# A fused attention and SwiGLU kernel: k and q of the fourth unit load ahead of the first weight slice, and the second slice loads and converts over more units

## The chip, the cores and the metric

The kernel runs on one core of a Trainium2 chip. Its engines are TensorE (PE, with its weight loads PEld), VectorE (DVE), ScalarE (ACT), GpSimd (POOL) and SyncE (SP), which here does nothing but start transfers. The metric is the device time of one execution in microseconds (us); lower is better.

## What is computed

Attention with a sigmoid in place of the softmax, over 4 batches of 12 heads, 448 tokens, 64 numbers a head; its result, as 1792 tokens of 768 numbers, goes through a root-mean-square norm and a SwiGLU layer. q, k and v are 32-bit floats; the weights arrive as 64-bit floats.

```python
def _attn_ref(q, k, v):
    scale = 1.0 / np.sqrt(q.shape[-1])
    scores = scale * np.matmul(q, k.transpose(0, 1, 3, 2)) - np.log(q.shape[2])
    return np.matmul(1.0 / (1.0 + np.exp(-scores)), v)

def _moe_ref(x, w_gate, w_val, w_out, rms_g):      # x: 1792 x 768
    xn = x / np.sqrt(np.mean(x * x, -1, keepdims=True) + 1e-06) * rms_g
    g = xn @ w_gate                                # 768 x 1536
    return (g / (1.0 + np.exp(-g)) * (xn @ w_val)) @ w_out
```

## The kernel before

**Attention.** The work is cut into 12 units, each of four heads of one batch (three units a batch), and each unit into 7 chunks of keys. The main loop (L897 to L919) takes two chunks a step, n = 0, 2, 4 and so on up to 84: `scores` (L265: 12 matmuls and one sigmoid on ACT for each chunk), then `av` (L284: 4 matmuls, each of two passes) of the two chunks before them. So unit u begins at chunk 7u. Below, "scores 4.0" is the first chunk of unit 4, and units count from 0: the fourth unit is unit 3.

**What a unit needs.** q and k are loaded as floats (`load_qk`, L191: two transfers of 224 KB each for q and two for k), split on DVE into a high and a low half of 16 bits (`qk_hi` L221, `qk_lo` L225), and transposed into `t_b`. Units 0 and 1 are transposed on PE; so is q of unit 2 (`on_pe`: matmuls at L257 into a PSUM tile `tr`, copied out by ACT at L262 and DVE at L260). From unit 3 on, and for k of unit 2, a DMA transposes them (L228, L234). `FILL` (L849) says in which chunk each of these steps is issued: while unit u computes, unit u + 2 is split and transposed, v of unit u + 1 and k and q of unit u + 4 are loaded. A matmul tile for `tr`, for `av`, for the norm's sums and for the later products comes from the same ring of four PSUM banks (`ps_m`), so a `tr` matmul waits until the one four banks earlier has been copied out.

**Weights.** The gate and value matrices are cut into 6 slices of 256 columns, 768 KB for each matrix of a slice. `load_w` (L451) queues three transfers a matrix (one of 384 KB and two of 192 KB); `run_load` (L458) starts the next one of that queue. `split_w` (L462) converts a slice: for each matrix three DVE passes over 64-bit words (L436, L437, L438), then four differences (L488), the 16-bit high half on ACT (L491) and the low half on DVE (L494). Its first list (`first`) has for slices 0 and 1 the gate's four entries, then the value's four and the differences; the last pass of a matrix queues the loads of the next slice, since its room is then free. `wr` in the profile is the room of the weights, `xc` holds loads of q and k, `t_b` and later the normed tokens.

**What sets the order.** Three lists (`adds`, `norms`, `splits`) are worked off by `run_later` (L797) within a credit for DVE and ACT that grows with every chunk; a part of `splits` runs only when nothing of the first two stands ready. The sums of squares are added on DVE (L314) and summed on PE (`ssq`, L346); the norm of a batch is then a row of small DVE instructions (L351 to L371), two spreads (L374), a product on PE (`rinv`, L384) that ACT copies (L385), the scaling (L388), sums (L410) and splits of the scaled tokens (L392, L395, L399). What is left at the end of attention is issued in a fixed number of parts before and within the first products.

**Transfers.** All of them are started by SP, in the order of the program. Eight completion semaphores are used in turn, so a transfer is started only when the one eight places ahead of it has landed, and when the room that it writes is free.

**After attention** come 24 blocks of products with the weights (`quad`, L535, matmuls at L524, tiles cb, cd, ca) and the products with w_out (L727), in which PE goes from one matmul to the next.

Of the kernel before, what the change touches and what calls it, by code (L numbers as in the profile page):

```python
# [24 lines left out]
def attention_then_swiglu(  # L25
# [42 lines left out]
    ps_m = ctx.enter_context(tc.tile_pool(name="ps_m", bufs=4, space=bass.MemoryType.PSUM))  # L68

    WARM, BETWEEN = 6, 2  # L70
    SPLIT_AT, REST_AT = (8, 30), 12
    LOADS_FROM = 10
    PIECES = (0, 4), (4, 3)
    MID = 3
    SLOT = 0.8
# [109 lines left out]
    def load(src, dst, u):  # L185
        b, n = divmod(u, NPAIR // 2)
        for r in range(2):
            rows = src[b, 4 * n + 2 * r : 4 * n + 2 * r + 2].rearrange("h s d -> (h s) d")
            nc.sync.dma_start(dst[:, r], rows.rearrange("(p c) d -> p c d", p=P))  # L189

    def load_qk(u, t):  # L191
        load((q, k)[t], (raw_b if u < 2 else ld_b)[u % 2][:, t], u)
# [13 lines left out]
    def g_columns():  # L206
        ps = bank("g")
        nc.tensor.matmul(ps[:, :NCC], g_row, ident[:NCC, :NCC], start=True, stop=True)
        nc.vector.tensor_copy(g_sb.rearrange("p (c o) -> p o c", o=2), ps[:, :NCC].rearrange("p (o c) -> p o c", o=2))
# [55 lines left out]
    def scores(u, c):  # L265

        T = t_b[u % 3]
        ps = banks("sc")

        for n, (l, m) in enumerate(PARTS):  # L270
            for r in range(2):
                rows = slice(D * r, D * r + D)
                for j in range(2):
                    cols = slice(PB * j, PB * j + PB)
                    o = ps[cols, r, :S].rearrange("p (c x) -> p c x", c=NSLOT)
                    nc.tensor.matmul(  # L276
                        o, T[rows, 1, l, c, cols], T[rows, 0, m, :, cols], start=(n == 0), stop=(n == 2)
                    )
        a = at[u, c] = a_b[(u * NSLOT + c) % 4]
        nc.scalar.activation(  # L280
            a, ps[:, :, :S], AF.Sigmoid, bias=-math.log(S), scale=1.0 / (math.sqrt(D) * SQ * SQ)
        )
# [39 lines left out]
    def run_evictions(n):  # L322
        for part in evictions[:n]:
            part()
        del evictions[:n]
# [123 lines left out]
    loads = []  # L449

    def load_w(fc, kind):  # L451


        src = swapped((w_gate, w_val)[kind][:, 2 * fc * P : 2 * fc * P + 2 * P])
        dst = raw_w[kind].rearrange("p c f w -> p c (f w)")
        loads.extend((fc, lambda d=d, x=x: nc.sync.dma_start(d, x)) for d, x in zip(sides(dst), src))

    def run_load():  # L458
        if loads:
            loads.pop(0)[1]()  # L460
# [331 lines left out]
    adds, norms, splits = [], [], []  # L792
# [4 lines left out]
    def run_later():  # L797
        calls[0] += 1
        credit[0] = min(credit[0] + SLOT, 2.5)
        credit[1] = min(credit[1] + ACT_SLOT, 0.6)  # L800
        for queue in (adds, norms, splits):
            while queue:
                part, cost, *on_act = queue[0]
                if part is wait:
                    if cost <= calls[0]:
                        queue.pop(0)
                    break
                if credit[bool(on_act)] <= 0:
                    break
                queue.pop(0)  # L810
                part()
                credit[bool(on_act)] -= cost
# [12 lines left out]
    K, Q = 1, 0  # L825
# [40 lines left out]
    with tc.manual_schedule():  # L866
# [16 lines left out]
        load_v(1)  # L883
        load_w(0, 0)
        load_w(0, 1)
        for t in (K, Q):
            for _ in range(3):
                run_load()
            load_qk(3, t)

        transpose_here(0, Q)
        warm(BETWEEN)
# [3 lines left out]
        split = {}  # L896
        for n in range(0, len(todo) + 2, 2):  # L897
            for u, c in todo[n : n + 2]:
                scores(u, c)
                run_evictions(1)  # L900
                for part in FILL[c]:
                    part(u)
                if n == 6 and c == 6:
                    g_columns()
                run_later()
            for u, c in todo[max(n - 2, 0) : n]:
                av(u, c)
                run_evictions(1)
                run_later()
            for _ in range(n // LOADS_FROM):  # L910
                if loads and loads[0][0] < 2:
                    run_load()
            if n in SPLIT_AT:
                fc = SPLIT_AT.index(n)
                split[fc] = split_w(fc)
                first, second = split[fc]
                splits.extend(first[:4] if fc == 0 else first + second)
            if n == REST_AT:
                splits.extend(split[0][0][4:] + split[0][1])  # L919
        run_evictions(len(evictions))  # L920


# [46 lines left out]
        for fc, n in order:  # L969
# [5 lines left out]
            elif fc + 1 < NFC:  # L975
                first, second = split[fc + 1] = split_w(fc + 1) if n == 0 else split[fc + 1]
# [97 lines left out]
```

## Time and profile before

| | |
|---|---|
| median of 3 runs | 575.09 us (572.03 to 577.34) |
| the profiled execution | 576.98 us, of which the span of its instructions 575.2 us |
| PE busy | 563.9 us (98%), 4230 matmuls |
| DVE, ACT busy | 437.8 us (76%), 265.9 us (46%) |
| transfers | 87.25 MB, mean 152 GB/s |

The span is what lies between the first and the last instruction; about 1.8 us of the execution lie around it. All times below are counted from the start of the span. PE busy is the sum of its matmuls at whatever clock was granted. The page also gives the granted TensorE clock in 40 slices of the span; all but the third show 9 tenths of full speed (the third shows 8).

### The profile page before, as it was taken

The page shows a single profiled execution, that of the slowest core. Times are in us where ns is not written, and L with a number is a line of the kernel's source. Part 1 is how long each engine was busy: PE and PEld are TensorE (multiplying, and loading weights), DVE is VectorE, ACT ScalarE, POOL GpSimd, SP SyncE. Part 2 cuts the span into 40 slices and gives each one's busy share as a digit, 9 for nine tenths or more (in the row PEclk, how much of TensorE's full clock was granted, in tenths as well). Part 3 has the DMA queues.
Part 4 walks back from the last instruction along what each step waited for, and adds up shares of the span by engine and source line. Part 5 has one row for each costly group of instructions (what it writes and reads, how often), then busy time and mean ns, then how long its engine had stood idle before and what let it go on. Part 6 is the DMA issues. An engine that isn't in the chain of part 4 may idle for free.

```text
span 575.2 us, 10261 instructions
## 1 busy us (share of the span) xinstructions
PE 563.9 (98%) x4230; PEld 304.4 (53%) x4230; DVE 437.8 (76%) x576; ACT 265.9 (46%) x397; POOL 0.7 (0%) x6
## 2 busy tenths in 40 slices
PE   8979999999999999999999999999999999999997
PEld 6435454454555555555555555555556666666664
DVE  4597899998887777878778787787557987777751
ACT  5759698886454243342433424325438342222220
POOL 0000000000000000000000000000000000000000
PEclk9989999999999999999999999999999999999999
DMA  7999999881016357282573835632526566444211
GB/s 246 216 272 264 245 228 256 167 189 20 1 46 169 120 156 197 90 226 79 155 192 98 219 81 156 189 106 65 179 59 224 152 217 201 145 142 145 71 43 41
DMA packets 98417, 87.25 MB, mean 152 GB/s; under 512 B 38719, under 2 KB 91458, under 8 KB 98370
## 3 DMA queue, kind: packets, MB, share of 16 engines
q1 hardware_dynamic: 97810, 85.91, 57.0%
q8 instruction: 33, 0.54, 0.4%
q10 hardware_dynamic: 560, 0.69, 0.3%
q14 instruction: 14, 0.11, 0.1%
HBM read 61.34 MB, written 16.52 MB: 135 GB/s over the span
## 4 chain that ended last, share of the span: by engine, by line
PE 85%; DMA 6%; DVE 4%; ACT 2%; SPq 1%; issue 1%; DVEq 0%; ACTq 0%
PE cb L524 28%; PE cd L524 14%; PE oc L727 7%; PE o L727 7%; PE od L727 7%; PE ca L524 7%; PE av L291 6%; PE sc L276 4%; PE ob L727 4%; DMA xc<-room 2%; DMA xc<-in_q_dram 1%; DMA wr<-in_moe_w_gate_dram 1%; ACT room L280 1%; DMA room<-in_k_dram 1%; SPq L189 1%
## 5 line engine op out<-in xcount | busy, mean ns | idle before, releaser
L524 PEld LDWEIGHTS <-wr 128*128 128x128 f16 x1512 | 147.8, 98 | 138.6 <-issue 1.0
L524 PE MATMUL cb<-xc,wr 128*128 128x448 f16 x756 | 147.3, 352 | 0.0
L280 ACT ACTIVATE room<-sc 128x896 f32<-128x896 f32 x84 | 75.4, 933 | 18.5 <-PE sc L276 17.8
L291 PE MATMUL av<-room 64*64 64x448 f32 x672 | 74.1, 548 | 0.2 <-DMA room<-in_v_dram 0.2
L524 PE MATMUL cd<-xc,wr 128*128 128x448 f16 x324 | 65.2, 352 | 0.0
L276 PE MATMUL sc<-xc 64*64 64x448 f16 x1008 | 58.5, 351 | 2.4 <-ACT room L280 1.6
L276 PEld LDWEIGHTS <-xc 64*64 64x64 f16 x1008 | 30.9, 107 | 34.4 <-issue 22.4
L579 DVE TENSOR_TENSOR room<-cd,room 128x448 f32<-128x448 f32 x24 | 15.0, 625 | 43.1 <-PE cd L524 43.1
L727 PEld LDWEIGHTS <-xc 128*128 128x128 f16 x360 | 35.2, 98 | 23.3
L494 DVE SCALAR_TENSOR_TENSOR wr<-wr 128x1536 f16<-128x1536 f32 (+3 forms) x28 | 37.3, 1355 | 12.2 <-ACT wr L491 12.2
L524 PE MATMUL ca<-xc,wr 128*128 128x448 f16 x216 | 44.8, 352 | 0.0
L727 PE MATMUL o<-room,wr 128*128 128x384 f16 x252 | 41.1, 326 | 0.0
L291 PEld LDWEIGHTS av<-room 64*64 64x64 f32 x672 | 26.2, 135 | 24.3 <-issue 19.0
L547 ACT ACTIVATE room<-cb 128x448 f32<-128x448 f32 x24 | 13.1, 544 | 53.8 <-PE cb L524 53.8
L568 ACT ACTIVATE room<-cb 128x448 f32<-128x448 f32 x24 | 13.1, 544 | 50.6 <-PE cb L524 30.6
L727 PEld LDWEIGHTS <-room 128*128 128x128 f16 x270 | 26.4, 98 | 17.5
L491 ACT ACTIVATE wr<-wr 128x768 f16<-128x768 f32 (+1 forms) x48 | 34.0, 761 | 0.0
L582 ACT ACTIVATE room<-room 128x448 f32<-128x448 f32 x24 | 13.8, 577 | 43.2 <-DVE room L579 43.2
L727 PEld LDWEIGHTS <-wr 128*128 128x128 f16 x252 | 24.7, 98 | 16.3
L682 ACT ACTIVATE xc<-xc 128x1536 f16<-128x1536 f32 (+1 forms) x12 | 14.5, 1260 | 36.0 <-DVE xc L679 36.0
L488 DVE TENSOR_TENSOR wr<-wr 128x384 f32<-128x384 f32 x48 | 26.5, 553 | 0.8
L540 ACT ACTIVATE room<-cb 128x448 f32<-128x448 f32 x24 | 13.1, 544 | 25.5 <-PE cb L524 25.5
(98 smaller groups left out, 679.1 us busy)
## 6 DMA issues: line engine op xcount, KB each, us to landing
y_d<-room SPq DMA_DIRECT2D x24, 448.0 KB, 3.3
xc<-in_moe_w_out_dram SPq DMA_DIRECT2D x12, 768.0 KB, 5.7
xc<-y_d SPq DMA_DIRECT2D x22, 384.0 KB, 4.3
room<-in_v_dram SPq DMA_DIRECT2D x24, 224.0 KB, 4.0
out_dram<-room SPq DMA_DIRECT2D x49, 96.0 KB, 2.2
wr<-in_moe_w_gate_dram SPq DMA_DIRECT2D x12, 384.0 KB, 4.0
wr<-in_moe_w_gate_dram SPq DMA_DIRECT2D x24, 192.0 KB, 4.8
wr<-in_moe_w_val_dram SPq DMA_DIRECT2D x12, 384.0 KB, 6.2
```

Source lines behind the costliest of these rows:

```text
L276: nc.tensor.matmul(o, T[rows, 1, l, c, cols], T[rows, 0, m, :, cols], start=(n == 0), stop=(n == 2))
L280: nc.scalar.activation(a, ps[:, :, :S], AF.Sigmoid, bias=-math.log(S), scale=1.0 / (math.sqrt(D) * SQ * SQ))
L291: nc.tensor.matmul(ps[D * (j ^ r) : D * (j ^ r) + D, :S], v_b[u % 2][rows, r, c], a[rows, r], start=(c == 0), stop=(c == NSLOT - 1),)
L488: first.append((lambda o=o, f0=f0, f1=f1: tt(wf[:, o], wf[:, f0], wf[:, f1], ALU.subtract), 0.6))
L491: nc.scalar.activation(t[:, 0, s], wf[:, s], AF.Copy, scale=SW)
L494: stt(t[:, 1, s], wf[:, s], SW, t[:, 0, s], ALU.mult, ALU.subtract)
L524: nc.tensor.matmul(ps, w[:, l, b, c], xc[n, a][:, r, c], start=(not more and c == 0 and m == 0), stop=(c == NK - 1 and m == 2), skip_group ...
L540: nc.scalar.activation(y[:, 0], pb[:, :S], AF.Copy)
L579: tt(y[:, 1], pd[:, :S], y[:, 1], ALU.add)
L582: nc.scalar.activation(y[:, 1], y[:, 1], AF.Silu, scale=UNIT)
L682: return lambda: nc.scalar.activation(s[:, 0, a:b], f[:, a:b], AF.Copy), 0.0, ()
L727: nc.tensor.matmul(ps[:, :HALF], a(m, l), w(m, r), start=(not more and m == 0 and n == 0), stop=(m == NM - 1 and n == 2), skip_group_check ...
```

## The change

Before the loop, k and q of unit 3 are queued ahead of the six transfers of weight slice 0, of which only the gate's three are started there; the other three follow at steps 0, 2 and 4. The transfers of slice 1 are started one at a time at steps 14, 18, 22, 26, 30 and 34 (before: one a step from 10, two a step from 20). Slice 0 is converted as before (the gate from step 8, the rest from 12); of slice 1 only the gate's conversion begins at step 30, and the value's, the differences and the halves at step 42. The amount of work and of bytes is the same.

```diff
-    SPLIT_AT, REST_AT = (8, 30), 12
-    LOADS_FROM = 10
+    SPLIT_AT = 8, 12, 30, 42
+    LOADS_AT = 0, 2, 4, 14, 18, 22, 26, 30, 34
...
-        for t in (K, Q):
-            for _ in range(3):
-                run_load()
-            load_qk(3, t)
+        load_qk(3, K)
+        load_qk(3, Q)
+        for _ in range(3):
+            run_load()
...
-            for _ in range(n // LOADS_FROM):
-                if loads and loads[0][0] < 2:
-                    run_load()
+            if n in LOADS_AT:
+                run_load()
             if n in SPLIT_AT:
-                fc = SPLIT_AT.index(n)
-                split[fc] = split_w(fc)
+                fc, rest = divmod(SPLIT_AT.index(n), 2)
+                if not rest:
+                    split[fc] = split_w(fc)
                 first, second = split[fc]
-                splits.extend(first[:4] if fc == 0 else first + second)
-            if n == REST_AT:
-                splits.extend(split[0][0][4:] + split[0][1])
+                splits.extend(first[4:] + second if rest else first[:4])
```

How the instructions move, at three places. First, SP's queue before the loop, from v of unit 1 (L189, `in_v_dram`) to the transpose of k of unit 2 (L234); `in_k_dram` and `in_q_dram` are unit 3's, `wr` is weight slice 0:

```order
 L189 DMA room<-in_v_dram 128x448 x2
+L189 DMA xc<-in_k_dram 128x448 x2
+L189 DMA xc<-in_q_dram 128x448 x2
 L456 DMA wr<-in_moe_w_gate_dram 128x3x256
 L456 DMA wr<-in_moe_w_gate_dram 64x3x256 x2
-L189 DMA xc<-in_k_dram 128x448 x2
 L456 DMA wr<-in_moe_w_val_dram 128x3x256
 L456 DMA wr<-in_moe_w_val_dram 64x3x256 x2
-L189 DMA xc<-in_q_dram 128x448 x2
 L234 DMA_TRANSPOSE xc<-room 128x14x128
```

q of unit 3 has moved past all six weight transfers, and k past three.

Second, SP's queue from the transpose of unit 3 (the first L228) to that of unit 4 (the second), between which stand k of unit 6, v of unit 3 and q of unit 6 and transfers of weight slice 1. Before:

```order
L228 DMA_TRANSPOSE xc<-room 128x28x128
L456 DMA wr<-in_moe_w_gate_dram 128x3x256
L456 DMA wr<-in_moe_w_gate_dram 64x3x256 x2
L189 DMA xc<-in_k_dram 128x448 x2
L189 DMA room<-in_v_dram 128x448 x2
L456 DMA wr<-in_moe_w_val_dram 128x3x256
L189 DMA xc<-in_q_dram 128x448 x2
L228 DMA_TRANSPOSE xc<-room 128x28x128
```

And now:

```order
L228 DMA_TRANSPOSE xc<-room 128x28x128
L456 DMA wr<-in_moe_w_gate_dram 128x3x256
L189 DMA xc<-in_k_dram 128x448 x2
L189 DMA room<-in_v_dram 128x448 x2
L189 DMA xc<-in_q_dram 128x448 x2
L228 DMA_TRANSPOSE xc<-room 128x28x128
```

Ahead of the transpose of unit 4 there now stands one weight transfer instead of four; two more follow ahead of that of unit 5, two ahead of that of unit 6, and the last one, with the first of slice 2, ahead of that of unit 7.

Third, DVE's queue at the end of attention. L388, L410, L395 and L399 belong to the norm of the third batch; the last two L314 are the adds after which PE can sum the squares of the fourth batch:

```order
+L314 TENSOR_TENSOR room<-room 128x448
+L388 TENSOR_TENSOR room<-room 128x1344 x2
+L314 TENSOR_TENSOR room<-room,xc 128x448
+L410 TENSOR_TENSOR room<-room 128x1344
 L395 CAST room<-room 128x1344
+L314 TENSOR_TENSOR room<-room 128x448
+L314 TENSOR_TENSOR room<-room,xc 128x448
 L399 TENSOR_TENSOR room<-room 128x1344
 L395 CAST room<-room 128x1344
-L314 TENSOR_TENSOR room<-room 128x448
-L314 TENSOR_TENSOR room<-room,xc 128x448
 L399 TENSOR_TENSOR room<-room 128x1344
```

The two adds now stand ahead of an L399, an L395 and an L399, where only one L399 followed them before. On PE, the third batch's `rinv` (L384) has moved back from behind the scores of chunk 11.1 to behind `av` of chunk 10.6.

## Rows read from the trace of the kernel before

**Rows 1.** Windows: us, PE, PEld, DVE, ACT, POOL busy, PEclk, DMA share, GB/s.
```profile
29.80:32.90 3.10, 0.00 (x0) 0.00 (x1) 3.00 (x5) 1.03 (x2) 0.00 (x0) 1.00 0.90 287
33.40:36.70 3.30, 3.30 (x22) 1.16 (x24) 3.07 (x6) 0.38 (x1) 0.00 (x0) 0.52 0.98 312
...
150.00:160.00 10.00, 10.00 (x55) 5.16 (x54) 8.06 (x10) 7.00 (x13) 0.00 (x0) 1.00 0.00 0
```
**Rows 2.** Timeline of PE around 33 us: start, duration, operation, count, [idle before].
```profile
32.92 0.60 PE L257 MATMUL tr<-room 128*128 128x128 f16 x6 [3.14 <-DVE xc L260]
33.45 3.26 PE L291 MATMUL av<-room 64*64 64x448 f32 x16
```
**Rows 3.** Timeline of DVE, 22 to 56 us.
```profile
22.19 0.62 DVE L221 TENSOR_SCALAR room<-xc 128x896 f16<-128x896 f32 x1
...
27.99 0.63 DVE L221 TENSOR_SCALAR room<-xc 128x896 f16<-128x896 f32 x1 [3.99 <-DMA xc<-in_q_dram]
...
29.73 0.56 DVE L436 TENSOR_SCALAR wr<-wr 128x768 uint32<-128x768 uint32 x1
...
32.19 0.68 DVE L260 CAST xc<-tr 128x512 f16<-128x512 f32 x1
...
55.47 0.63 DVE L221 TENSOR_SCALAR room<-xc 128x896 f16<-128x896 f32 x1 [1.84 <-DMA xc<-room]
```
**Rows 4.** Timeline of SP: start and duration of the issues.
```profile
11.55 2.41 SPq L456 DMA_DIRECT2D wr<-in_moe_w_gate_dram  x3
...
18.09 1.67 SPq L189 DMA_DIRECT2D xc<-in_q_dram  x2
...
46.28 5.45 SPq L228 DMA_TRANSPOSE xc<-room  x1
...
57.35 6.73 SPq L228 DMA_TRANSPOSE xc<-room  x1
```
**Rows 5.** Waits of SP, 45 to 52 us: total, times, longest.
```profile
SPq L228 <- DMA wr<-in_moe_w_gate_dram: 1.0, 1, 1.0
```
**Rows 6.** Timeline of PE, 55 to 88 us.
```profile
55.84 1.33 PE L276 MATMUL sc<-xc 64*64 64x448 f16 x24
...
61.80 1.34 PE L291 MATMUL av<-room 64*64 64x448 f32 x10 [0.22 <-DMA room<-in_v_dram]
...
67.69 0.76 PE L276 MATMUL sc<-xc 64*64 64x448 f16 x12 [0.35 <-DMA xc<-room]
...
87.10 1.57 PE L276 MATMUL sc<-xc 64*64 64x448 f16 x24 [0.70 <-ACT room L280]
```
**Rows 7.** Timeline of PE, 130 to 147 us.
```profile
130.22 0.55 PE L384 MATMUL rinv<-room,ones 112*128 112x448 f16 x2
...
131.29 1.67 PE L291 MATMUL av<-room 64*64 64x448 f32 x16
...
141.93 0.95 PE L346 MATMUL ssq<-ones,room 128*112 128x1 f32 x8 [0.37 <-DVE room L314]
...
146.13 0.73 PE L384 MATMUL rinv<-room,ones 112*128 112x448 f16 x2
```
**Rows 8.** Timeline of DVE, 131 to 147 us.
```profile
131.78 1.56 DVE L388 TENSOR_TENSOR room<-room 128x1344 f32<-128x1344 f32 x1 [2.92 <-ACT room L385]
...
138.28 1.56 DVE L399 TENSOR_TENSOR room<-room 128x1344 f16<-128x1344 f32 x1
139.76 0.85 DVE L395 CAST room<-room 128x1344 f16<-128x1344 f32 x1
...
141.25 0.62 DVE L314 TENSOR_TENSOR room<-room,xc 128x448 f32<-128x448 f32 x1
...
143.26 0.15 DVE L351 TENSOR_SCALAR m<-ssq 112x4 f32<-112x4 f32 x1
...
145.84 0.62 DVE L374 TENSOR_TENSOR room<-ident,yl 112x448 f16<-112x448 f32 x1
```
**Rows 9.** Timeline of ACT: the last square of attention.
```profile
140.23 0.54 ACT L308 ACTIVATE xc<-av 128x448 f32<-128x448 f32 x1
```

## The prediction

> **What bounds the kernel now.** I read four views in this order. The windows first: from about 150 us on TensorE is busy 10.00 of every 10 us at full granted clock [rows 1], so nothing that the change moves can shorten that part; what can move is the attention stage, up to some 147 us. [...]
>
> [...] The second half of unit 2's q waits 3.14 us for L260 on DVE, and the 16 `av` matmuls behind it take 3.26 us [rows 2] where 16 such take 1.67 at full clock [rows 7]. So the hole costs 3.14 + 1.59 = 4.7 us.
>
> Third, DVE, to see why L260 was late. It stood idle 3.99 us until q of unit 3 had landed, at 27.99; behind that L221 stand in DVE's order the L225 of the same unit and the gate's three passes from 29.73, and only then L260 at 32.19 [rows 3]. Last, SP's own queue: q of unit 3 was issued at 18.09, behind the whole first weight slice, whose gate transfers begin at 11.55 [rows 4]. The bound of this stretch is thus one late load, through three engines.
>
> Smaller losses follow. PE waits 0.22 us for a v load and 0.35 us for the transpose of unit 5, and 0.70 us for ACT at 87.10 [rows 6]; at the end `ssq` waits 0.37 us for DVE [rows 7].
>
> **The early part.** Work and bytes stay the same; only positions change. Up to v of unit 1, SP queues eight loads of 2 x 224 KB, 3.7 MB; before, three weight transfers (0.8 MB), k, three more and q follow. k was ready for the L221 at 22.19, which did not wait [rows 3], with 4.9 MB queued up to it. In the new order q of unit 3 closes at 4.6 MB, so I estimate it before 22.2 us, while DVE comes to it at 24.0 (27.99 - 3.99). The gate then closes at 5.4 MB; between 4.9 MB at 22.2 and 6.2 MB at 28.0 that is an estimated 24.3. Without the wait DVE ends unit 3's q at about 25.7 and turns to the gate then: 1.4 us to spare. L260 would be free at 32.19 - 3.99 = 28.2, before its matmuls; I leave 0.2 us of wait. With the hole goes the low clock behind it. Gain: 3.14 - 0.2 + 1.59 = 4.5 us; bounds 0 (gate as late as q was) and 4.7.
>
> **Is the gain kept up to unit 4?** PE then comes to scores 4.0 at 55.84 - 4.5 = 51.3 [rows 6]. Those need the transpose of unit 4, issued at 46.28 [rows 4] and landed by 55.47, when DVE's L221, which overwrites its source, was released [rows 3]: 9.2 us from issue to landing. It must come over 4 us earlier, or the gain is handed back there. In SP's order two gate pieces and one of the value have gone from in front of it, and its 1.0 us of waiting for a gate piece [rows 5] goes with them, since its eighth predecessor is now the transpose of unit 3. That one gains too, as does DVE, whose splits it needs. I take 42 us, 4.3 earlier, and landing at 51.2; 0.2 us of wait, bounds 0 and 4.5.
>
> [...]
>
> For units 5 to 7 there are now eight transfers between one transpose and the next (k, v, q of two each, and two weight pieces). So the second q transfer waits until the last transpose has landed, and the next transpose follows directly. At 9.2 us of landing and 0.9 for q, a unit takes 10.1 us; PE took 11.85 from unit 4 to unit 5 (55.84 to 67.69), of which the two transfer waits [rows 6] and the `ssq` and `rinv` products are part. The transposes then fall at 51.9 and 62.0 for units 5 and 6 and land at about 61.1 and 71, so unit 5 no longer waits. Of the losses between 60 and 68 us, 0.57 us are plain waits; the two waits also break up the pairs of chunks around them, which makes about 1.9 in all by the starts of the steps. I take 1.0 us of gain; bounds 0 and 1.9.
>
> **Slice 1 converts later.** Its value passes, differences and halves shift by up to two units, and the norm of the first batch comes ahead of them. Nothing needs slice 1 before the second product block, beyond 150 us, so by itself this costs nothing: the norm's instructions fill the place. ACT's 0.70 us of wait may go or double; I take 0, bounds -0.7 and +0.7. If DVE lost this cover, PE would stand at `rinv` of the second batch.
>
> **The end of attention.** The later conversion pushes the third batch's norm back on DVE. `rinv` now stands behind `av` of 10.6: half of the 1.67 us of the row at 131.29 comes ahead of it, and ACT does one 0.54 us square first, so the scaling that began at 131.78 begins about 1.2 us later, at 133.0 [rows 7, 8]. From there DVE does, before the two last L314, two L388, an L410, one L314 and an L395. The first two and L399 pass the same 128 x 1344 words, 1.48 us from one start to the next (138.28 to 139.76); with 0.55 and 0.8 for the short ones that makes 5.8: free at 138.8. But the adds need the last squares, which ACT ends at 140.77 [rows 9], so DVE idles nearly 2 us, which before it filled with L399 and L395 at 138.28 and 139.76 [rows 8]. The adds end at about 141.45, which removes the 0.37 us wait of `ssq`. Behind them come now L399, L395 and L399: 1.48 + 0.8 + 1.48 = 3.8 us, to 145.2, and L351 began at 143.26: 1.9 us later. The chain from L351 to the second L374 is unchanged, so its end moves from 146.4 to 148.3. `rinv` of the last batch, which PE reached at 146.13 just in time [rows 7], now waits some 2 us. Cost at the first product behind it: +1.9; bounds 0.5 (if DVE runs ahead through the time won earlier) and 3.5 (if the low clock that followed the 3.14 us hole follows this one too, at the same 1.6).
>
> **Sum.** -4.5 + 0.2 - 1.0 + 0 + 1.9 = -3.4 us. Against the profiled execution: 576.98 - 3.4 = 573.6 (its span 575.2 to 571.8). That execution lies 1.9 us above the median of 575.09, so in terms of the median: 571.7 us, 0.6% less.
>
> **The rivals.**
>
> B, the transfer queue sets the pace, and the change ends slower. Place: SP, from unit 5 to 7, where eight transfers tie each transpose to the landing of the last. Price: the transpose of unit 5, issued at 57.35, released PE only at 67.69 [rows 4, 6], 10.3 us; with 0.9 for q that is a period of 11.2. From 42.0 the transposes of units 5, 6 and 7 would then land at 63.5, 74.7 and 85.9, where PE, 4.5 us ahead, wants them at 62.8 (67.34 - 4.5) and then every 10.0 us (scores 7.0 are the second half of the row at 87.10, some 20 us behind scores 5.0), at 72.8 and 82.8: 3.1 us are given back by unit 7. With the end's +1.9 and the 4.5 it gives +0.5 us; if the transpose of unit 4 does not come earlier either, all 4.5 go back at once, and +1.9 to +3.5 us remain. 575.6 to 578.6. It decides where a landing takes longer than about 9 us. For it: 10.3 in the trace. Against it: those 10.3 came with all of slice 1 queued, and the queue is emptier now.
>
> C, the whole gain and a free end: DVE reaches the end with time in hand, because its 2.92 us wait [rows 8] is slack, and both transfer and ACT waits go. -4.7 - 1.9 - 0.7 - 0.3 = -7.6: 567.5 us. Against it: DVE's order at the end hangs on PE's `rinv` and on ACT's last squares, not on how early it was before.
>
> D, the hole stays: the gate lands as late as q did, L436 waits in L221's place and L260 stands behind it as before. For it: the gate's room of 1.4 us is small and estimated. Then 0 to -2 us early and +1.9 at the end: 575.0 to 577.0.
>
> **Chances.** Forecast 0.50 (its own range 569.5 to 574), B 0.20, C 0.20, D 0.10. The runs before spread over 5 us, and about 1%, 5.8 us, is what a measurement of this kernel can tell from no change. Faster by over 1%, below 569.3: most of C and a little of the forecast, 0.21. Slower by over 1%, above 580.8: only B with more low clock than counted, 0.04. Within 1%: 0.75. The range for 8 in 10 holds the forecast, D, most of B and half of C: 567 to 577.5.
>
> **What would show it.** Right: no wait of PE at L257, the granted clock at 1.0 between 28 and 40 us, no idle DVE before unit 3's q; scores 4.0 near 51 us; the transpose of unit 4 issued near 42; DVE idle of 1 to 2 us ahead of the last two L314, and a wait of PE of about 2 us at the last `rinv`. Wrong: a wait of L436 for the gate (D); waits of PE for transposes in units 4 to 7 (B); or a last `rinv` that does not wait (C).

## The result, and the profile after

The changed kernel is slower: 577.89 us (median of 19 runs, 574.36 to 581.14) against 574.41 us of the kernel before in the same session (19 runs, 572.03 to 577.98). The ratio is 1.0063, with a 95% interval of 1.0047 to 1.0080: 0.6%, or 3.5 us. Forecast were 571.7 us and a range up to 577.5: the result lies just above the range, and the change goes the other way.

The profiled execution of the changed kernel took 574.36 us, the shortest of its 19, with a span of 572.6 us. That of the kernel before took 576.98, longer than 17 of the 19 runs it was now measured with. So the two profiles alone say "2.6 us faster", and the medians say "3.5 us slower". What the profile can show is where the work moved; what the change is worth has to come from more than two executions.

**What came as forecast.** The timeline of PE over the stretches of [rows 2, 6, 7] (start, duration, line, operation, count, [idle before]):

```profile
29.79 0.52 PE L257 MATMUL tr<-room 128*128 128x128 f16 x6
30.24 1.73 PE L291 MATMUL av<-room 64*64 64x448 f32 x16
...
51.10 1.33 PE L276 MATMUL sc<-xc 64*64 64x448 f16 x24
...
143.38 0.36 PE L384 MATMUL rinv<-room,ones 112*128 112x448 f16 x1 [2.05 <-DVE room L374]
143.91 0.35 PE L384 MATMUL rinv<-room,ones 112*128 112x448 f16 x1 [0.17 <-DVE room L374]
144.09 1.87 PE L524 MATMUL ca<-xc,wr 128*128 128x448 f16 x9
```

The wait at L257 is gone, and the 16 `av` matmuls behind it take 1.73 us, not 3.26. The scores of chunk 4.0 start at 51.10, where 51.3 was worked out. At the end the last `rinv`, which had no wait before, now waits 2.05 + 0.17 us; "some 2 us" was forecast.

SP's timeline, against [rows 4]: the transposes of units 4 and 5.

```profile
40.33 5.69 SPq L228 DMA_TRANSPOSE xc<-room  x1
...
51.37 5.43 SPq L228 DMA_TRANSPOSE xc<-room  x1
```

Both are issued about 6 us earlier than before; 42 had been worked out for the first. From the waits of PE over the whole span (what waits, for what: total us, times, longest):

```profile
PE rinv L384 <- DVE room L374: 2.2, 2, 2.0
PE sc L276 <- ACT room L280: 1.5, 3, 0.6
...
PE sc L276 <- DMA xc<-room: 0.2, 1, 0.2
```

Waits for transposes are 0.2 us in all (0.35 before), and there is none for a v load (0.22 before). The one large wait is the new one. The timeline of DVE over the stretch of [rows 8] shows how it comes about:

```profile
132.35 0.85 DVE L395 CAST room<-room 128x1344 f16<-128x1344 f32 x1
135.55 0.62 DVE L314 TENSOR_TENSOR room<-room 128x448 f32<-128x448 f32 x1 [2.35 <-ACT room L308]
136.28 0.63 DVE L314 TENSOR_TENSOR room<-room,xc 128x448 f32<-128x448 f32 x1
136.82 1.55 DVE L399 TENSOR_TENSOR room<-room 128x1344 f16<-128x1344 f32 x1
138.29 0.85 DVE L395 CAST room<-room 128x1344 f16<-128x1344 f32 x1
139.18 1.56 DVE L399 TENSOR_TENSOR room<-room 128x1344 f16<-128x1344 f32 x1
140.65 0.15 DVE L351 TENSOR_SCALAR m<-ssq 112x4 f32<-112x4 f32 x1
...
143.24 0.62 DVE L374 TENSOR_TENSOR room<-ident,yl 112x448 f16<-112x448 f32 x1
```

DVE idles 2.35 us ahead of the last adds, because ACT has not yet made the squares. Only then does it do L399, L395 and L399, which stand ahead of L351 in its queue, and `rinv` hangs on the end of that chain. Before, an L399 and an L395 filled this hole [rows 8].

One more wait stands in neither of these views. It is in the timeline of PE's weight loads:

```profile
126.29 0.19 PEld L291 LDWEIGHTS av<-room 64*64 64x64 f32 x4 [0.37 <-issue]
127.31 0.14 PEld L291 LDWEIGHTS av<-room 64*64 64x64 f32 x2 [0.83 <-ACT room L385]
```

Behind the third batch's `rinv`, at its new place inside `av` of 10.6, the next `av` stand 0.83 us for ACT's L385, which reads that `rinv` product and has an L308 ahead of it on ACT. The kernel before has no such wait in this stretch. PE's own timeline shows it only as six `av` matmuls that take 1.62 us, and the list of PE's waits not at all.

So nearly every sign that the prediction named for "right" is in this profile (only DVE's idle time is longer, 2.35 us, where 1 to 2 was named), and the time still went the other way. Two questions follow. What is the early gain worth in an ordinary execution? And does the end cost only the 2.2 us of wait?

### The profile page after: what moved, and what is told of

The parts are those of the page before. It is cut to its first block, busy times and chain, and to the rows that moved or that the text cites. A ratio compares the mean times of both kernels' runs of the same rounds, so it can differ in the third digit from the quotient of the medians.

```text
span 572.6 us, 10263 instructions
## 1 busy us (share of the span) xinstructions
PE 562.6 (98%) x4230; PEld 307.6 (54%) x4230; DVE 437.7 (76%) x576; ACT 265.7 (46%) x397; POOL 0.7 (0%) x6
## 4 chain that ended last, share of the span: by engine, by line
PE 92%; ACT 3%; DVE 3%; issue 1%; DVEq 0%; ACTq 0%
PE cb L524 28%; PE cd L524 14%; PE av L291 9%; PE oc L727 7%; PE o L727 7%; PE od L727 7%; PE ca L524 7%; PE sc L276 7%; PE ob L727 4%; ACT room L280 2%; PE tr L246 1%; PE warm L872 1%; PE tr L257 1%; DVE room L399 1%; PE ssq L346 0%
## 5 line engine op out<-in xcount | busy, mean ns | idle before, releaser
L276 PEld LDWEIGHTS <-xc 64*64 64x64 f16 x1008 | 33.2, 106 | 31.6 <-issue 20.5
L291 PEld LDWEIGHTS av<-room 64*64 64x64 f32 x672 | 27.7, 133 | 21.6 <-issue 16.3
L540 ACT ACTIVATE room<-cb 128x448 f32<-128x448 f32 x24 | 13.1, 544 | 25.5 <-PE cb L524 25.5
```

The costliest lines, as they stand in the source:

```text
L276: nc.tensor.matmul(o, T[rows, 1, l, c, cols], T[rows, 0, m, :, cols], start=(n == 0), stop=(n == 2))
L291: nc.tensor.matmul(ps[D * (j ^ r) : D * (j ^ r) + D, :S], v_b[u % 2][rows, r, c], a[rows, r], start=(c == 0), stop=(c == NSLOT - 1),)
L540: nc.scalar.activation(y[:, 0], pb[:, :S], AF.Copy)
```

## The experiments

The theory behind them: the early gain is smaller in most executions than in the profiled one, because the hole at L257, PE's 3.14 us wait and the slow `av` behind it [rows 2], varies (V in the expectations); and the wait at the end, which DVE's idle time causes (T, later put more narrowly as I), costs more than its length, if the low clock often follows it. Against V stands S: the hole is the same in every execution. The rival of T is X: the end is cheap, and transfers give back the early lead, in units 3 to 8. All ratios are to the kernel before on the same chip; where two ratios from different chips are compared, it is assumed that they would be the same on one.

| run | median us (runs) | before | ratio [95%] |
|---|---|---|---|
| before_again | 573.05 (1) | 574.15 | |
| after_again | 574.66 (1) | 574.15 | |
| front_only | 573.50 (10) | 574.15 | 0.9989 [0.9974, 1.0003] |
| late_only | 578.02 (4) | 574.15 | 1.0060 [1.0038, 1.0083] |
| held_back | 578.06 (7) | 574.53 | 1.0052 [1.0033, 1.0071] |
| conv_early | 583.34 (5) | 574.53 | 1.0160 [1.0139, 1.0181] |
| filled_wait | 576.47 (12) | 574.53 | 1.0042 [1.0023, 1.0062] |
| adds_behind | 574.53 (12) | 574.12 | 1.0007 [0.9991, 1.0022] |
| adds_no34 | 573.63 (12) | 574.12 | 1.0000 [0.9986, 1.0015] |
| spread_24 | 573.18 (12) | 574.12 | 0.9988 [0.9973, 1.0002] |
| half_at_40 | 573.77 (12) | 574.36 | 0.9996 [0.9978, 1.0015] |
| half_at_36 | 572.34 (12) | 574.36 | 0.9963 [0.9947, 0.9979] |

### Both kernels profiled once more

The two kernels with no edit, one execution each.

> The kernel before, unchanged, for the profile of a second execution. Theory V (the hole before unit 3's q varies from one execution to the next, and the profiled execution of before, 2.6 us above the median of its 19 runs, had an unusually large one): PE waits well under 3 us at L257, the granted clock does not fall behind it, and the time is near 574.4. Theory S (the hole is the same in every execution): the wait is again 3.0 to 3.3 us with the low clock behind it.

> The changed kernel, unchanged, for the profile of a second execution; its profiled one was the shortest of 19, 3.5 us under their median. Theory T (the wait at the last rinv and what follows it): the wait of some 2 us is there again and the granted clock falls behind it, 1.7 us more than in the first profile. Theory X (transfers): waits for transposes or for v in units 4 to 8 that the first profile did not have, 2 to 4 us together.

The timeline of PE in the second execution of the kernel before, at the place of [rows 2]:

```profile
31.35 0.50 PE L257 MATMUL tr<-room 128*128 128x128 f16 x6 [1.48 <-DVE xc L260]
31.78 1.74 PE L291 MATMUL av<-room 64*64 64x448 f32 x16
```

The wait is there, but it is 1.48 us, not 3.14, and the clock does not fall behind it: it is 1.00 from 30 to 40 us, and 16 `av` matmuls take 1.74 us. The program is the same, but q of unit 3 landed at 26.3 us in this execution and at 27.9 in the first. The 4.7 us hole of the profile that I read was that execution's, not the kernel's.

In the second execution of the changed kernel the last `rinv` waits 2.2 us again, with the clock at 1.00 from 144 to 152 us, behind it, so T came only in part. Nor did X's 2 to 4 us come: the transpose of unit 7 costs PE 0.90 us, where it cost 0.22. At 574.66 us this execution too is far below the median of the 19.

Unit by unit (first scores), the changed kernel's first profile leads the second one of before by 1.5 us at unit 2 (31.80 against 33.33), by 2.5 at unit 5 (61.25 against 63.76) and by 1.8 at unit 11. Then it loses in two steps. The lines on which they rest, of PE in the second execution of before,

```profile
122.97 1.30 PE L276 MATMUL sc<-xc 64*64 64x448 f16 x24
...
135.74 1.88 PE L524 MATMUL cb<-xc,wr 128*128 128x448 f16 x9
...
142.77 1.86 PE L524 MATMUL ca<-xc,wr 128*128 128x448 f16 x9
```

and in the first of the changed kernel (its first `ca`, at 144.09, is shown above):

```profile
121.17 1.31 PE L276 MATMUL sc<-xc 64*64 64x448 f16 x24
...
134.99 1.88 PE L524 MATMUL cb<-xc,wr 128*128 128x448 f16 x9
```

The 96 scores, 80 `av` and two `rinv` matmuls up to the first `cb` product take 12.77 us in the kernel before (122.97 to 135.74) and 13.82 in the changed one (121.17 to 134.99): the 1.05 us of the split `av`. From there to the first `ca` product it is 7.03 us before and 9.10 now: 2.07 for the last `rinv`. The changed kernel is now 1.3 us behind (144.09 against 142.77), and the spans, 572.6 and 571.3, differ by the same 1.3: from the first `ca` on, every profile without a low clock there takes 428.5 us. Between these two executions, which have no low clock at these places, the early part gains 1.8 us and the end loses 3.1.

### The early part alone

```diff
-        for t in (K, Q):
-            for _ in range(3):
-                run_load()
-            load_qk(3, t)
+        load_qk(3, K)
+        load_qk(3, Q)
+        for _ in range(6):
+            run_load()
```

The loop stays as in the kernel before: the loads of slice 1, and the conversions, at their old steps.

> Only k and q of unit 3 ahead of weight slice 0; all else as before. Theory S: 4 to 5 us faster than before. Theory V: 0 to 2 us faster, since a typical execution of before has little of the hole. If the queue then gives it back (rival B of the prediction): no change, with waits for the transposes of units 4 and 5 in the profile.

Measured was 0.9989, no clear difference: S's 4 to 5 us are excluded, V's lower part and B's "no change" are not. PE's timeline has no wait at L257, but three others behind it:

```profile
40.56 0.76 PE L276 MATMUL sc<-xc 64*64 64x448 f16 x12 [0.69 <-DMA xc<-room]
...
46.04 1.24 PE L291 MATMUL av<-room 64*64 64x448 f32 x6 [1.32 <-DMA room<-in_v_dram]
...
53.75 1.33 PE L276 MATMUL sc<-xc 64*64 64x448 f16 x24 [0.81 <-DMA xc<-room]
```

Two transposes and a v load take back 2.8 us between 40 and 54 us. So transfers do give the lead back where the transfers of slice 1 stay crowded: the mechanism of rival B, in units 3 and 4, and with the old spread. The two halves of the change belong together: the new spread is what keeps the lead up to unit 4.

### The loop alone

The changed kernel with the prologue of the kernel before:

```diff
-        load_qk(3, K)
-        load_qk(3, Q)
-        for _ in range(3):
-            run_load()
+        for t in (K, Q):
+            for _ in range(3):
+                run_load()
+            load_qk(3, t)
```

> Only the spread transfers and the later conversion of slice 1; the order before the loop as before. Theory T: 2 to 4 us slower than before, with the wait at the last rinv. If the spread itself gains what it takes from the waits between 60 and 68 us: 1 us less than that. Theory X: no slower than before, since it is PE's lead from the early part that runs into the transfers.

1.0060, the whole loss of the changed kernel. The timeline of PE at the end:

```profile
142.91 1.87 PE L524 MATMUL cd<-xc,wr 128*128 128x448 f16 x9
146.83 0.36 PE L384 MATMUL rinv<-room,ones 112*128 112x448 f16 x1 [2.05 <-DVE room L374]
147.36 0.35 PE L384 MATMUL rinv<-room,ones 112*128 112x448 f16 x1 [0.17 <-DVE room L374]
147.54 3.31 PE L524 MATMUL ca<-xc,wr 128*128 128x448 f16 x9
```

and its windows (columns as in [rows 1]):

```profile
143.00:147.00 4.00, 1.95 (x11) 0.80 (x10) 3.66 (x14) 0.54 (x1) 0.00 (x0) 1.00 0.00 0
147.00:151.00 4.00, 3.83 (x12) 1.50 (x11) 3.97 (x4) 0.54 (x1) 0.00 (x0) 0.60 0.02 4
```

The same wait as in the changed kernel, to a hundredth; but here the clock is 0.60 in the 4 us that follow, and nine `ca` matmuls take 3.31 us where they took 1.87. This is what the first profile of the changed kernel does not show. Over its 19 runs it is usual: in 13 the mean granted clock of the whole execution is 0.997 or less, in 6 it is 0.999 or 1.0. The median of the 13 is 578.23 us, that of the 6 is 576.85 us. So the low clock costs some 1.4 us where it comes, and without it the changed kernel still lies 2.4 us above the 574.41 of before. A mean over the execution does not say where the clock was low: the kernel before, too, has 0.997 or less in 16 of the 83 executions that the sessions below list. The run with the filled wait, below, settles the place.

This kernel has its own L257 wait (1.4 us), and PE also waits 2.1 us for v of unit 6. In both profiles of the changed kernel that wait is absent; it comes and goes between the profiles below (1.5 us in filled_wait, 1.7 in half_at_40).

### The norm behind the last chain

The changed kernel, with L399, L395 and L399 of the third batch moved behind the chain from L351 to L374:

```diff
-        while len(later) > N_NORM:
+        while len(later) > N_NORM + 3:
...
+        held, later[:3] = later[:3], []
+        later[8:8] = held
```

> The changed kernel, but the three instructions of the third batch's norm that stand between the last adds and the last norm's chain on DVE (L399, L395, L399) are held back behind that chain. Theory T (the wait at the last rinv and the low clock that it often brings are what the change costs): the wait falls from 2.2 us to under 0.3, no low clock behind it, and the time is 574 to 575, within 0.2% of before. Theory X (waits for v and for transposes in units 4 to 8 are the cost): the wait goes, but the time stays above 576, 0.4% or more slower than before.

The wait at `rinv` goes, and the kernel stays about as slow, 1.0052. By the number this is what X expected; the profile shows why it is not X. The timeline of DVE,

```profile
137.54 0.63 DVE L314 TENSOR_TENSOR room<-room 128x448 f32<-128x448 f32 x1 [2.35 <-ACT room L308]
...
139.93 0.16 DVE L351 TENSOR_SCALAR m<-ssq 112x4 f32<-112x4 f32 x1 [1.04 <-PE ssq L346]
```

that of ACT,

```profile
151.14 1.51 ACT L392 ACTIVATE xc<-room 128x448 f16<-128x448 f32 x3 [3.45 <-DVE room L388]
```

and that of PE:

```profile
153.13 3.47 PE L524 MATMUL cb<-xc,wr 128*128 128x448 f16 x9 [2.61 <-ACT room L540]
```

The three norm instructions now delay the L388 of the fourth batch. ACT's L392 waits 3.45 us for that, L540 stands behind it on ACT, and PE waits 2.61 us for L540 ten microseconds later. The clock falls there too: it is 0.83 from 150 to 160 us, and nine `cb` matmuls take 3.47 us. So "the three instructions are in the way of `rinv`" was too narrow. I read these rows so that DVE has no slack left in this stretch: the 2.35 us in which it does nothing (with 1.04 more here) are lost, and only the place at which PE pays for them has moved. What counts would then be the idle time ahead of the adds, not what stands behind them; the run with the adds put back, below, tries that.

### Slice 1 converted whole at step 30

```diff
-                splits.extend(first[4:] + second if rest else first[:4])
+                if fc == 0:
+                    splits.extend(first[4:] + second if rest else first[:4])
+                elif not rest:
+                    splits.extend(first + second)
```

> The changed kernel, but slice 1 converts whole from step 30, as before; its loads stay spread and the order before the loop stays new. DVE's order is then that of before. Theory T: no wait at the last rinv, 573 to 574.5, the same as before or up to 0.2% faster. Theory X: the spread loads still cost, over 576.

A miss: 1.0160, from a place that none of the theories spoke of. DVE's timeline,

```profile
73.05 0.56 DVE L436 TENSOR_SCALAR wr<-wr 128x768 uint32<-128x768 uint32 x1 [12.63 <-DMA wr<-in_moe_w_val_dram]
```

ACT's,

```profile
79.72 1.04 ACT L392 ACTIVATE xc<-room 128x448 f16<-128x448 f32 x2 [10.10 <-DVE room L388]
```

and SP's:

```profile
63.28 6.33 SPq L228 DMA_TRANSPOSE xc<-room  x1
69.66 0.62 SPq L456 DMA_DIRECT2D wr<-in_moe_w_val_dram  x1
```

The value's first pass stands 12.63 us in DVE's queue for the value's last transfer, and ACT and PE stand behind it; PE waits 10.1 us for ACT. That transfer stands on SP behind the transpose of unit 6, and is issued at 69.66. (A conversion, when it begins, starts what is left of its slice. So the gate's at step 30 starts this sixth transfer of slice 1, and the table's step 34 starts the first of slice 2; the description of the change gives step 34 for the sixth.) The end cannot be judged from this run. It shows the tie between the two tables instead: with loads spread this far, a value's conversion that begins at 30 holds up DVE, ACT and PE.

### The wait filled with idle matmuls

The changed kernel; ten matmuls, whose result nothing reads, go into an unused half of a PSUM tile ahead of the last `rinv`:

```diff
+        if (fc, n) == (0, 0):
+            for _ in range(10):
+                nc.tensor.matmul(both_d[:, 1, :S], ones16, xc[0, 5][:, 0, 0], start=True, stop=True)
```

> The changed kernel with ten more matmuls (into an unused bank, 1.9 us at full clock) in the first product block, just ahead of the last rinv, so that PE works while DVE is late; they compute nothing that is used. If the low clock follows from PE's idling there: the granted clock is 1.0 in nearly every run and the time falls by 1 to 1.5 us against the changed kernel, to 0.35 to 0.5% slower than before, with rinv no earlier. If the low clock has another cause: no change, 0.6% slower, and runs at 0.997 as often as not.

The timeline of PE at this place:

```profile
143.63 2.06 PE L555 MATMUL cd<-xc,ones 128*128 128x448 f16 x10
145.84 0.36 PE L384 MATMUL rinv<-room,ones 112*128 112x448 f16 x1 [0.16 <-DVE room L374]
```

PE is busy for the 2 us in which it stood, and `rinv` comes no sooner: in this profile as in the first of the changed kernel it starts 21.6 us behind the first scores of unit 11 (124.20 here, 121.74 there). The ratio falls to 1.0042, 0.2% or 1.2 us below the changed kernel's, and 11 of the 12 runs have a mean clock of 0.999 or 1.0, where 6 of 19 had it. So the low clock goes with PE's idle time at this place: 13 of 19 runs with it have a mean of 0.997 or less, 1 of 12 without it. The intervals of the two ratios overlap, so the size is rough; the 1.4 us between the two groups of runs above agree with it.

This profile also shows what the two of the changed kernel do not. Its program is the same up to this place, but PE waits for transfers ahead of it, for the transpose of unit 5 (0.56 us) and for v of unit 6:

```profile
79.29 0.98 PE L291 MATMUL av<-room 64*64 64x448 f32 x8 [1.46 <-DMA room<-in_v_dram]
```

Its time, 576.83 us, is near the median of its runs; the two profiles of the changed kernel are over 3 us below the median of the 19.

### The last adds put back

The changed kernel, with only DVE's order ahead of the last adds as it was: these two stand behind L399 and L395 of the third batch again.

```diff
+        held, norms[:] = at_once(norms), []
+        while len(held) > 1:
+            held.pop(0)[0]()
...
-        later = at_once(splits + norms)
+        later = at_once(splits + held + norms)
```

> The changed kernel, but at the end of attention the last two adds stand again behind an L399 and an L395 of the third batch's norm, as before, so that DVE has work while it waits for the last squares; the norm itself stays late, and nothing else moves. Theory I (what the later conversion costs at the end is DVE's idle time ahead of those adds, some 2 us, which PE pays back at the last rinv or, when the chain is freed there, one block later): the wait at rinv falls to 0.3 to 0.8 us, no other takes its place, no low clock in most runs, 574.5 to 575.8. Theory X (late transfers): still 576.5 or more.

The timeline of DVE, against the one of the changed kernel above:

```profile
132.98 0.85 DVE L395 CAST room<-room 128x1344 f16<-128x1344 f32 x1
133.87 1.56 DVE L399 TENSOR_TENSOR room<-room 128x1344 f16<-128x1344 f32 x1
135.35 0.85 DVE L395 CAST room<-room 128x1344 f16<-128x1344 f32 x1
136.18 0.63 DVE L314 TENSOR_TENSOR room<-room 128x448 f32<-128x448 f32 x1
136.91 0.63 DVE L314 TENSOR_TENSOR room<-room,xc 128x448 f32<-128x448 f32 x1
137.45 1.55 DVE L399 TENSOR_TENSOR room<-room 128x1344 f16<-128x1344 f32 x1
138.92 0.15 DVE L351 TENSOR_SCALAR m<-ssq 112x4 f32<-112x4 f32 x1
```

DVE no longer idles ahead of the adds, L351 begins at 138.92 where it began at 140.65, and no wait of PE at `rinv` is left. The time is that of the kernel before, 1.0007 [0.9991, 1.0022], and 11 of the 12 runs have a mean clock of 0.999 or 1.0. All else of the change is in place, and the loss is gone, so the idle time ahead of the adds carries it. The sizes agree: from 1.0063 to 1.0007 are 3.2 us, and 2.07 of wait with 13/19 of 1.4 for the clock make 3.0. What stays here is the stall behind the third `rinv`: the 0.83 us stand in this run's weight loads too, and its stretch up to the first `cb` takes 13.82 us (121.80 to 135.62). With it the early lead ends as 0.4 us at the first `ca` (142.37 against 142.77).

### Without the load at step 34

The kernel above with LOADS_AT ending at 30, so that one load, the first of slice 2, is left out of the loop's table:

```diff
-    LOADS_AT = 0, 2, 4, 14, 18, 22, 26, 30, 34
+    LOADS_AT = 0, 2, 4, 14, 18, 22, 26, 30
```

> As the run with the adds behind, and without the load at step 34, so that the first transfer of slice 2 no longer stands in SP's queue ahead of k, v and q in unit 4. Theory X: the waits for v of unit 6 and for the transpose of unit 7 shrink, 1 us faster than the run with the adds behind. If that transfer is harmless: no change, within 0.4 us.

1.0000 [0.9986, 1.0015], not to be told from the kernel above by the intervals. But this does not decide between the two expectations: the median is 0.9 us lower (573.63 against 574.53), near X's 1 us, and the 0.53 us that PE waits for the transpose of unit 7 in the profile of adds_behind are gone here.

### A spread that ends at step 24

The prologue of the change, loads two steps apart, and slice 1 converted whole from step 30, as in the kernel before:

```diff
-    LOADS_AT = 0, 2, 4, 14, 18, 22, 26, 30, 34
+    LOADS_AT = 0, 2, 4, 14, 16, 18, 20, 22, 24
...
+                if fc == 0:
+                    splits.extend(first[4:] + second if rest else first[:4])
+                elif not rest:
+                    splits.extend(first + second)
```

> k and q of unit 3 ahead as in the changed kernel, slice 1 spread over steps 14 to 24 only, and converted whole from step 30 as before, so that DVE's order is that of before everywhere. If the early part is worth what the hole of a typical execution shows and the spread keeps the transposes in time: no wait at L257, none of over 0.5 us for transfers, 572.5 to 573.5, 0.2 to 0.4% faster than before. If the shorter spread brings the transfer waits of the run with the early part alone: 573.5 to 574.5, no change.

0.9988 [0.9973, 1.0002]: the end is as before and there is no wait at `rinv`, but of the early lead little is left, and the result lies between the two expectations. At unit 4 (51.40) this run leads the second profile of before by 1.7 us, at unit 5 (63.28 against 63.76) by 0.5. With slice 1's transfers closer together the lead goes in unit 4.

### The later conversion at step 40, and at step 36

One number of the changed kernel, and then two tables:

```diff
-    SPLIT_AT = 8, 12, 30, 42
+    SPLIT_AT = 8, 12, 30, 40
```

> The changed kernel with one number altered: the rest of slice 1 converts from step 40 instead of 42. The transfers' order stays that of the change; the norm of the third batch comes two positions earlier and stands at the end of attention as in the kernel before. Theory I (the whole loss is DVE's idle time before the last adds, which the order at the end decides): no wait at the last rinv, and the lead of some 1.8 us that the changed kernel has at unit 11 is kept to the first product block: 572.3 to 573.5, 0.1 to 0.3% faster than before. If the spread or the later conversion costs by itself: 574 or more.

```diff
-    SPLIT_AT = 8, 12, 30, 42
-    LOADS_AT = 0, 2, 4, 14, 18, 22, 26, 30, 34
+    SPLIT_AT = 8, 12, 30, 36
+    LOADS_AT = 0, 2, 4, 14, 18, 20, 24, 26, 28
```

> k and q of unit 3 ahead; slice 1's transfers at steps 14, 18, 20, 24, 26 and 28, none of slice 2 in attention, and the rest of slice 1 converted from step 36; the order at the end of attention is that of before. Theory I: as with step 40, and up to 0.5 us better if the waits for v of unit 6 and for the transpose of unit 7 go with the later transfers: 572 to 573.3. If the transfers then crowd unit 5 instead: 573.5 to 574.5, no change.

At 40 the ratio is 0.9996: the loss is gone by one number, but the gain that was expected (572.3 to 573.5) is not there at 573.77. The order at the end is again that of the kernel before, on DVE (L399 and L395 ahead of the last adds) and on PE (the third `rinv` behind scores of 11.1): no wait at the last `rinv`, none for L385, and 12.77 us up to the first `cb` (124.07 to 136.84). Between 40 and 42 both orders tip. PE waits 1.7 us for v of unit 6 in this profile, which is where the lead goes.

At 36, with the six transfers of slice 1 done by step 28 and none of slice 2 in the table, the kernel is faster than both: 572.34 us, ratio 0.9963 [0.9947, 0.9979], 2.0 us below the kernel before. From the waits of PE in its profile:

```profile
...
PE av L291 <- DMA room<-in_v_dram: 0.8, 1, 0.8
PE ssq L346 <- DVE room L314: 0.4, 1, 0.4
PE sc L276 <- DMA xc<-room: 0.2, 1, 0.2
```

No wait at L257 or at `rinv`, and less for v (0.8 us, of unit 5) than at 40; the stretch up to the first `cb` is 12.77 us (122.58 to 135.35). That is the change's early part with the end of the kernel before. How much of the 2.0 us comes from less waiting for v and how much from the hole that is gone was not tried apart.

## Why the prediction was wrong

Two steps of the sum failed: the first term, which was three times too large, and the end, which left out a wait of PE and the low clock. From -3.4 to +3.5 are 6.9 us. The lead at unit 11 was forecast at 4.5 - 0.2 + 1.0 = 5.3 us and is an estimated 0.7: 4.6 of them. The end was forecast at 1.9 and costs about 4.1: 2.2.

**The hole was sized from one execution (the larger failure).** The first term, 4.5 us, took the 3.14 us wait and the low clock behind it, 0.52 over 3.3 us [rows 1, 2], for the kernel's. Its mechanism is right: the wait is gone, the clock is 1.00 from 28 to 40 us, and the scores of 4.0 start at 51.10, for 51.3 worked out. But the kernel before waits 1.48 us at this place in its second profile, and late_only, with the same prologue, 1.4; neither is followed by a low clock (1.00 from 30 to 40 and from 30 to 38 us). In these two executions the term is some 1.5 us, 3.0 less than forecast. A warning stood in the numbers: the profiled execution lay 1.9 us above the median of three, and 2.6 above that of 19. I subtracted these 1.9 us from both kernels, as if they would stay. In part they look like the very hole that the change removes, so the gain was to be cut by them.

**Up to unit 4 the lead is kept**, as forecast. The transpose of unit 4 was issued at 40.33, for 42 forecast, and PE does not wait for it. front_only shows what the spread does for that: without it 2.8 us go to transfers in units 3 and 4.

**The transfer waits of 60 to 68 us** are gone in both profiles of the changed kernel, against 0.57 us before. The lead of its first profile over the second one of before grows from 1.5 us at unit 2 to 2.5 at unit 5, so the 1.0 us taken is what these two profiles show. But then the lead shrinks, and for that the forecast had nothing. Five profiles have the changed kernel's program up to unit 11 (its own two, adds_behind, held_back, filled_wait). Against the second profile of before they lead by 2.4 us in the mean at unit 5, by 1.6 at unit 7, by 0.8 at unit 8 and by 0.7 at unit 11 (there 1.8, 1.5, 1.2, -0.2, -0.7). What is lost up to unit 7 is lost in executions in which PE waits for transfers, as filled_wait shows; why these waits come and go stays open.

**Slice 1 converts later: not quite nothing.** No DVE wait for slice 1 came of it, and conv_early shows that with this spread the later conversion is even needed. ACT's wait of 0.70 us at 87.10 is gone, and 0.61 at 69.95 has come. But in unit 7 these five profiles take 12.2 to 13.0 us from the first scores to those of unit 8, and both profiles of before 11.62: 0.8 us more in the mean. In the first profile 0.29 us of it are `ssq` waiting for DVE's L314; the rest was not tried apart.

**The end was forecast at 1.9 us and costs about 4.1.** Its first part held: 2 us of DVE idle ahead of the adds were worked out (2.35 measured) and some 2 us of wait at the last `rinv` (2.22 measured, 2.07 in the sum of the stretch). Two things were wrong. The low clock was only the upper bound, 3.5; it comes in about 13 of 19 runs, so some 1.0 us of it belonged in the cost. I had one row to judge by, a 3.14 us wait with low clock behind it, and treated a 2 us wait as safe with no row that said so. And a wait was missed: the prediction saw that the third `rinv` moves into `av` of 10.6 and that ACT does a square ahead of L385, and followed this to DVE only. PE's own next `av` wait for that L385 as well: the stretch is 1.05 us longer, of which the wait explains 0.83. All seven profiles with `rinv` at this place have the 0.83 us for L385 (both of the changed kernel, late_only, held_back, filled_wait and the two with the adds put back); the ones with the old order have none. It was not taken away by itself: half_at_40, which is without it, and adds_behind, which has it, differ by 0.6 us, and their intervals overlap.

**The sum again**, by the profiles without low clock: -1.8 at unit 11 against the second profile of before, +1.05 and +2.07 at the end; with 1.4 x 13/19 = 1.0 for the clock this makes +2.3. Measured is +3.5 (2.7 to 4.6 by the interval). But the 1.8 is again read from one execution, the shortest of 19: the fault of the prediction once more. With the 0.7 us that the five profiles lead by in the mean the sum is an estimated +3.4. It is good to about 1 us, since on the other side stands one profile of before, 1.1 us below the median of its session. So rival X has a share: transfers and unit 7 take back most of the lead. That the end's order carries the loss does not hang on this: filled_wait gets back 1.2 us, adds_behind a further 2.0 (1.0042 to 1.0007), and with the order of the end as before the kernel is equal (half_at_40) or faster (half_at_36).

**The rivals.** B came nearest: its range (575.6 to 578.6) is the only one that holds the result, and it had the sign. Part of its mechanism came too. SP's transposes of units 4 to 7 come 11.0, 10.5 and 10.6 us apart in the first profile (40.33, 51.37, 61.91, 72.49), between the 10.1 that I took and B's 11.2; PE waits only 0.2 us for them there, because they started earlier. In filled_wait's execution the first distance is 12.25 (41.04, 53.29), and PE does wait. But up to unit 7 B's 3.1 us are some 0.8 in the mean, and the larger share of the loss is at the end. C is excluded by the wait at `rinv`, D by the hole that is gone. The case that came was none of them whole: a first term near a third of the forecast, a part of B, the end near its large bound, and one wait more.

## What to carry to other kernels

Before a hole of the profile is entered as a gain, compare the profiled execution with the median: one that lies above it may owe its excess to that hole, and a second profile of the same kernel shows whether the hole is always there. The same holds for a lead that is read from the changed kernel's profile. Look for ready work that stands behind a waiting instruction: here DVE waited 2.35 us for ACT with an L399, an L395 and an L399 behind; moving these further back only moved PE's wait (2.22 us at `rinv`, 2.61 for L540 in held_back), and putting two of them ahead left none at `rinv` (adds_behind). Read the weight loads too: the 0.83 us that PE waited behind the moved third `rinv` showed as a wait only there. When a table of steps sets such an order by what happens to be pending, try the neighbouring values: from 42 to 40 the whole loss went here.

## What the runs showed of the hardware

The low clock followed a wait of PE in some executions and not in others: behind the same wait of 2.05 + 0.17 us the clock was 1.00 in two profiles of the changed kernel and 0.60 over 4 us in late_only, and of 19 executions of the changed kernel 13 had a mean clock of 0.997 or less and 6 of 0.999 or 1.0. Waits of 1.48 and 1.4 us at L257 did not bring it (1.00, and 16 `av` in 1.74 us, behind either); the 3.14 us wait did (0.52 over 3.3 us, and 16 `av` in 3.26); each is one execution. With PE kept busy by matmuls of no use through the 2 us wait, 11 of 12 executions had a mean clock of 0.999 or 1.0, where 6 of 19 had; that was worth about 0.2% of the whole kernel, with intervals that overlap.
